# Output projections in the scores' single PSUM bank, maxima products and transposes in the triple, two products moved ahead of the scores

## The chip, the cores and the metric

The kernel runs on one core of one Trainium2 chip. A core has five engines that each work through a queue of their own in order: PE (TensorE, matrix products, with its weight loads shown as PEld), DVE (VectorE), ACT (ScalarE), POOL (GpSimd) and SP (SyncE), which here only issues the DMAs. PE writes its results to PSUM, eight banks of 512 float32 values on each of 128 partitions; DVE and ACT read them from there. The metric is the time of one execution in device microseconds. Before the change the median of three runs was 2083.55 us (2079.57 to 2088.34).

## The reference

Four layers in a row on one sequence of 2048 rows of 448 values: attention, feed-forward, attention, feed-forward, each behind a layer norm without weights and with a residual sum. The attention has 16 heads of 28 and one key and one value head for all; the feed-forward has 1792 hidden values. Both attentions share their weights, and so do both feed-forwards.

```
    def _A_ref(x, wq, wk, wv, wo):
        B, S, D = x.shape
        H = 16
        Dh = D // H
        q = (lambda x, *d: x.transpose(*d))((x @ wq).reshape(B, S, H, Dh), 0, 2, 1, 3)
        k = x @ wk
        v = x @ wv
        scores = jnp.einsum("bhqd,bkd->bhqk", q, k) * (Dh ** -0.5)
        p = _softmax(scores, axis=-1)
        o = jnp.einsum("bhqk,bkd->bhqd", p, v)
        return (lambda x, *d: x.transpose(*d))(o, 0, 2, 1, 3).reshape(B, S, H * Dh) @ wo
    def _B_ref(x, w_gate, w_up, w_down):
        g = _silu(x @ w_gate)
        u = x @ w_up
        return (g * u) @ w_down
    x = A_x
    x = x + _A_ref(_layernorm(x, axis=-1), A_wq, A_wk, A_wv, A_wo)
    x = x + _B_ref(_layernorm(x, axis=-1), B_w_gate, B_w_up, B_w_down)
    x = x + _A_ref(_layernorm(x, axis=-1), A_wq, A_wk, A_wv, A_wo)
    x = x + _B_ref(_layernorm(x, axis=-1), B_w_gate, B_w_up, B_w_down)
    return x
```

## The kernel before

The sequence is cut into four chunks of 512 rows (c = 0 to 3) and sixteen blocks of 128 keys (kt = 0 to 15). Products that must be precise are made of a high and a low part of each operand: three products of float32r values for one. All engines' orders are written out by hand: the order of the Python calls is the order of each engine's queue, and the framework adds the waits.

The function `forward` is called twice, with `full` false and, under a condition at the end that does not hold here, with `full` true. What follows is the first call.

**Projection stage (`project`, `q`, `finish`).** For each chunk four projections follow each other in the order `TURN`: first the one with the keys and values (m = 3), then the queries (m = 0, 1, 2), sixteen in all, counted by `seen`. Each is eleven matmuls in one of the banks 0 to 3. ACT copies the result, POOL (or, for m = 3, DVE at L453) takes the low half, and SP writes both halves to a DRAM tile `qd`; for m = 3 it also writes the keys (L131) and, from a DVE transpose into tile `sg` (L466), the values `vsb` (L468). The copies go through a ring of three buffers called `halves`. Ahead of each chunk's projections `turned` transposes the normalised rows `xn` of that chunk on PE (`flip`, L248); ACT and DVE take the transposes out of PSUM. For the last chunk the norm is applied (L230) behind projection 8 in layer 0, where `seen` is 8, and in layer 1 ahead of it; its transposes stand ahead of projection 11.

**Stacks.** A group i = (c, g) is one chunk of queries by four of the heads; there are sixteen in a layer. `stack(i)` reads the group's queries from `qd` into one of three tiles `qts` with four DMAs (L346). Stacks 0 and 1 are issued during the projections of chunk 0 and 1 (through the list `waiting`, one per projection), the others in the scores, at kt = 4 of two groups earlier.

**Maxima (`quick_steps`).** For each group a bound on the scores is taken: one product of the stacked queries with a few keys (`kdiag`, L362), a DVE transpose into `sg` (L364), a reduction (L366), a split in high and low (L368, L369), a transpose (L371), a cast into tile `down` (L373), and a DMA (L131) that writes the result into four rows of the group's `qts` tile. `down` and `sg` have one buffer each. The step of group 0 is run inside projection 7 by `tick`, which is called after every matmul of a projection and takes a step at every second call once `ready` allows it (`open`: when `seen` is over 6). The step of group i + 1 is run in group i.

**Scores (`scores`).** The eight banks are dealt anew: two triples (`threes`, three banks each, one tile each), bank 6 for the output of the attention, bank 7 as the single bank. One `step(n)` is one group by one block of keys: twelve score matmuls (L529), three banks of one triple and bank 7 for the fourth head, then two exps on ACT, first of bank 7 (`pt1`, L535), then of the triple (`pt`, L536). The triples take turns, bank 7 is used in every step. After each step comes `between_steps(n)`, then `pv(n - 2)`, the products of the exps with the values (L558). `between_steps` puts in what has to be done beside the scores, using the triple that the next step will write (`free`): at kt = 10 the maxima step of the next group in bank 0 of `free` and, where the list `todo` has some, an output projection (`outproj`: twelve matmuls at L515 and a DVE add into the residual at L519) in bank 1; from group 12 on a further output projection at kt = 13. In group 9, at kt = 4, 6, 8 and 10, it also puts in the transposes for the feed-forward's first chunk (`flip`, k = 0 to 3, in bank 2 of `free`), which DVE takes out in two passes (L251, L252; for k = 3 L255, L261).

`todo` gets the four projections of a chunk a few steps after the chunk's last group: of chunk 0 in group 4, of chunk 1 in group 8, of chunk 2 in group 12. So groups 4 to 11 have one at kt = 10, groups 12 and 13 have one at kt = 10 and one at kt = 13. Chunk 3's come after the scores.

**Feed-forward (`FeedForward`)** follows; in layer 0 it runs the first projections of the next attention between its last units.

## Time and profile before

| what | value |
|---|---|
| median of the runs | 2083.55 us |
| profiled execution, its own time | 2082.46 us |
| its span | 2080.7 us |
| PE busy | 2020.0 us |
| ACT busy | 1298.5 us |
| mean granted TensorE clock | 0.996 |
| maxima products in the scores | 30, in the projection stages 2 |
| output projections in the scores | 24 |
| scores, first step of layer 0 and of layer 1 on PE | 67.98 us and 1095.92 us |

The page gives busy times by engine, the chain that ended last, and groups of instructions by line, engine and tile. In a line of the timeline the first number is the start in us from the span's start, the second the duration in us, then engine, line, operation, tiles and shapes. A bracket at the end gives how long the engine sat idle before it and what ended that. In SP's lines the time is that of issuing, not of the transfer, and "x4" means four in a row. Ends of matmuls are modelled; starts are what the argument goes by.

### The profile page before, as it was taken

To read this page: it belongs to the slowest core of one execution; us is meant where nothing else is said; L and a number is where in the kernel's file an instruction comes from. 1 tells how busy PE (TensorE), PEld (TensorE's weight loads), DVE (VectorE), ACT (ScalarE), POOL (GpSimd) and SP (SyncE) were. 2 spreads that over 40 slices of the span, in tenths; PEclk is the share of its full clock that TensorE was granted. 3 is DMA by queue.
4 is the path that set the end of the run, shared out by engine and by line. 5 is a ranking of instruction groups with operands and counts; after the bars stand their busy time and mean duration, and the time that the engine had idled before them with its cause. 6 is when DMAs were issued, how large, how long until landed. Compare 5 with 4: busy or idle time off the path is not lost.

```text
span 2080.7 us, 43770 instructions
## 1 busy us (share of the span) xinstructions
PE 2020.0 (97%) x18577; PEld 1302.4 (63%) x18577; DVE 510.1 (25%) x1038; ACT 1298.5 (62%) x2126; POOL 493.3 (24%) x504
## 2 busy tenths in 40 slices
PE   7999999999999999999999999999999999999998
PEld 5433333333348999999883333333333589999997
DVE  6111112211114322223450110112121152223222
ACT  3799898788883333333338999897888643333332
POOL 5211101012202333332341110110222123333321
PEclk9999999999999999999999999999999999999999
DMA  6311010021100111100142110101121001111102
GB/s 197 104 36 36 20 27 20 16 45 31 36 7 23 30 30 30 30 16 26 36 130 64 30 38 16 30 16 30 31 42 24 12 18 31 30 30 30 30 2 74
DMA packets 86591, 78.24 MB, mean 38 GB/s; under 512 B 26736, under 2 KB 66032, under 8 KB 86384
## 3 DMA queue, kind: packets, MB, share of 16 engines
q1 hardware_dynamic: 86384, 75.33, 13.3%
q8 instruction: 148, 2.42, 0.5%
q14 instruction: 59, 0.48, 0.1%
HBM read 51.51 MB, written 18.61 MB: 34 GB/s over the span
## 4 chain that ended last, share of the span: by engine, by line
PE 51%; ACT 40%; DVE 3%; issue 2%; DMA 2%; SPq 1%; POOL 1%; ACTq 0%; DVEq 0%; POOLq 0%
PE bank L293 38%; ACT pt L536 27%; ACT pt L535 12%; PE three L515 3%; PE bank L271 3%; PE bank L558 2%; PE three L529 2%; PE bank L515 1%; PE three L362 1%; PE bank L248 1%; DVE sg L364 1%; DMA o<-rd 1%; DVE xl L252 1%; DVE stats L217 0%; SPq L131 0%
## 5 line engine op out<-in xcount | busy, mean ns | idle before, releaser
L536 ACT ACTIVATE pt<-three 128x1536 f32<-128x1536 f32 x512 | 741.6, 1448 | 0.0
L558 PE MATMUL bank<-pt,vsb 128*32 128x512 f32 x4096 | 545.9, 605 | 0.6 <-ACT pt L536 0.6
L529 PEld LDWEIGHTS three<-qstack,keys 32*128 32x128 f32 x4608 | 252.3, 183 | 454.7 <-ACT pt L535 388.2
L529 PE MATMUL three<-qstack,keys 32*128 32x512 f32 x4608 | 498.2, 425 | 7.5 <-DVE xl L252 3.5
L529 PE MATMUL bank<-qstack,keys 32*128 32x512 f32 x1536 | 492.0, 425 | 0.0
L293 PE MATMUL bank<-xh,wgh 64*128 64x512 f32 x1728 | 450.8, 390 | 0.5
L535 ACT ACTIVATE pt<-bank 128x512 f32<-128x512 f32 x512 | 306.1, 598 | 117.4 <-PE bank L529 115.9
L293 PE MATMUL bank<-xh,wgl 64*128 64x512 f32 x1404 | 369.7, 388 | 0.0
L293 PE MATMUL bank<-wdh,h 64*128 64x448 f32 x1792 | 335.2, 363 | 1.2 <-ACT h L767 0.9
L293 PE MATMUL bank<-xl,wgh 64*128 64x512 f32 x1296 | 335.0, 387 | 0.0
L293 PEld LDWEIGHTS bank<-xh,wgh 64*128 64x128 f32 x1728 | 267.7, 184 | 8.6 <-DVE xl L252 1.6
L592 POOL TENSOR_TENSOR o<-o 128x512 f32<-128x512 f32 x32 | 41.1, 1284 | 910.7 <-DMA o<-rd 649.7
L293 PEld LDWEIGHTS bank<-wdh,h 64*128 64x128 f32 x1792 | 249.0, 185 | 8.0 <-issue 2.5
L685 POOL TENSOR_TENSOR xres<-stage,xres 128x448 f32<-128x448 f32 x112 | 131.1, 1192 | 489.8 <-ACT stage L684 489.8
L529 PEld LDWEIGHTS bank<-qstack,keys 32*128 32x128 f32 x1536 | 243.6, 183 | 1.4 <-ACT pt L535 1.2
L300 ACT COPY seen<-bank 128x1 f32<-128x1 f32 x664 | 81.0, 164 | 239.7 <-PE bank L293 238.3
L293 PEld LDWEIGHTS bank<-xh,wgl 64*128 64x128 f32 x1404 | 220.8, 184 | 3.7
L293 PE MATMUL bank<-wdl,h 64*128 64x448 f32 x896 | 218.2, 365 | 0.0
L765 ACT ACTIVATE sg<-bank 128x512 f32<-128x512 f32 x112 | 67.1, 599 | 220.6 <-PE bank L293 211.1
L293 PEld LDWEIGHTS bank<-xl,wgh 64*128 64x128 f32 x1296 | 200.8, 185 | 2.7
L766 DVE TENSOR_TENSOR sg<-bank,sg 128x512 f32<-128x512 f32 x112 | 77.5, 692 | 495.1 <-ACT sg L765 486.1
L558 PEld LDWEIGHTS bank<-pt,vsb 128*32 128x32 f32 x4096 | 80.8, 108 | 186.3 <-issue 171.4
(115 smaller groups left out, 1723.0 us busy)
## 6 DMA issues: line engine op xcount, KB each, us to landing
qstack<-qd SPq DMA_DIRECT2D x128, 112.0 KB
qd<-q SPq DMA_DIRECT2D x24, 512.0 KB
o<-rd SPq DMA_DIRECT2D x32, 256.0 KB
wdr<-in_B_w_down_dram SPq DMA_DIRECT2D x28, 224.0 KB
wr<-in_B_w_gate_dram SPq DMA_DIRECT2D x28, 192.0 KB
wr<-in_B_w_up_dram SPq DMA_DIRECT2D x28, 192.0 KB
keys<-q SPq DMA_DIRECT2D x32, 112.0 KB
out_dram<-xres SPq DMA_DIRECT2D x16, 224.0 KB
```

What stands on the lines that cost most here:

```text
L271: nc.tensor.matmul(po, a, b, start=(i == 0), stop=(i == len(seq) - 1))
L293: nc.tensor.matmul(po, a, b, start=start, stop=stop, skip_group_check=True)
L300: nc.scalar.copy(seen[:, i : i + 1], po[:, 0:1])
L515: nc.tensor.matmul(po[:, 0:D], a[:, g, ts_], b[:, g, :], start=(g + z == 0), stop=(g == NG - 1 and z == 2))
L529: nc.tensor.matmul(three[:, j, :] if j < 3 else one, k[js, ks], q[js, part, :], start=(z == 0), stop=(z == 2), tile_position=(32 * j, 0),)
L535: nc.scalar.activation(pt1, one, AF.Exp, scale=SCALE)
L536: nc.scalar.activation(pt, three, AF.Exp, scale=SCALE)
L558: nc.tensor.matmul(accs[i][32 * j : 32 * j + 32, :], vsb[:, kt, :], pts[n][j], start=(kt == 0), stop=(kt == NT - 1), skip_group_check=True,)
L592: nc.gpsimd.tensor_tensor(rb, oraw, rb, ALU.mult)
L685: nc.gpsimd.tensor_tensor(r, s, r, ALU.add)
L765: nc.scalar.activation(sg, pg[0], AF.Silu)
L766: nc.vector.tensor_tensor(sg, pg[1], sg, ALU.mult)
```

## The change

There are five edits.

1. At kt = 10 the output projection goes to bank 7 (`one`) instead of bank 1 of the free triple; those at kt = 13 go to bank 0 of the triple.
2. The reading of the maxima product (now `rows`) and of the transposes (now `flipped`) is put on a list `behind` when in the scores. At kt = 10 PE's queue then has product, transposes, projection in this order, and DVE's has the maxima chain, the transposes' two passes, and the projection's add.
3. The transposes k = 0 to 3 move from kt = 4, 6, 8 and 10 of group 9 to kt = 10 of the groups 9, 10, 11 and 12.
4. The maxima steps of groups 0, 1 and 2 are all run in the projection stage, from projection 8 on (`seen` over 7) instead of that of group 0 in projection 7; in the scores the steps begin at group 2 (for group 3).
5. For that, stack 2 is issued in the projection stage too, behind the DMAs of projection 4, instead of at kt = 4 of group 0.

```
-    def flip(got, tiles, ks=range(4), place=None):
+    def flip(got, tiles, ks=range(4), place=None, behind=None):
...
+            if behind is None:
+                flipped(tiles, k, pt, nc.vector.tensor_copy if place is not None else nc.scalar.copy)
             else:
+                behind.append(lambda k=k, pt=pt: flipped(tiles, k, pt, nc.vector.tensor_copy))
+
+    def flipped(tiles, k, pt, copy):
+        xh, xl, xd = tiles
+        if k < 3:
+            copy(xh[:, k, :], pt)
+            nc.vector.tensor_tensor(xl[:, k, :], pt, xh[:, k, :], ALU.subtract)
+            return
+        if xd is None:
+            copy(xh[:, k, :], pt)
+            high = xh[64:128, k, :]
...
+        nc.vector.tensor_tensor(xh[64:128, k, :], pt[64:128, :], high, ALU.subtract)
...
             def one():
                 pm = self.mbank()[1]
                 nc.tensor.matmul(pm, kd.rearrange("p j k -> p (j k)"), q[:, 0, :], start=True, stop=True)
+                if self.lent is None:
+                    rows(pm)
+                else:
+                    self.behind.append(lambda: rows(pm))
+
+            def rows(pm):
                 side = pers.tile([P, 512], F32, name="sg")
                 nc.vector.transpose(side, pm)
...
-            if c == 0 and m < 2:
+            if c == 0 and m < 3:
                 self.waiting.append(lambda: self.stack(m))
...
-                self.ready = NM if self.seen > 6 else 0
+                self.ready = 3 * NM if self.seen > 7 else 0
...
-            self.advance(len(self.steps), NM + KC * LEAD if full else NM)
+            self.advance(len(self.steps), NM + KC * LEAD if full else 3 * NM)
...
                     free = threes[(n + 1) % 2]
+                    one = free[:, 1, :] if full else banks[7]
                     self.lent = free[:, 0, :]
-                    if full or kt == 10:
+                    if full or kt == 10 and i > 1:
                         self.advance(KC if full else 1)
...
-                    if todo and (kt == 10 or kt == 13 and i > 11):
-                        todo.pop(0)(free[:, 1, :])
-                    if i == 9 and kt in (4, 6, 8, 10):
-                        flip(got, X0, [kt // 2 - 2], free[:, 2, :])
+                    if kt == 10 and 8 < i < 13:
+                        flip(got, X0, [i - 9], free[:, 2, :], self.behind)
+                    while self.behind:
+                        self.behind.pop(0)()
+                    if todo and kt == 10:
+                        todo.pop(0)(one)
+                    elif todo and kt == 13 and i > 11:
+                        todo.pop(0)(free[:, 0, :])
...
-                    if kt == 4 and i + 2 < len(GR):
+                    if kt == 4 and 2 < i + 2 < len(GR):
                         self.stack(i + 2)
```

More of the change, by code (lines that the diff above doesn't have):

```diff
@@ L240, in norm @@
         return got
-    def flip(got, tiles, ks=range(4), place=None):
-        xh, xl, xd = tiles
+    def flip(got, tiles, ks=range(4), place=None, behind=None):
         for k in ks:
@@ L248, in flip @@
                 nc.tensor.transpose(pt[:, P * t : P * t + P], got["x"][:, t, P * k : P * k + P], ident)
-            copy = nc.vector.tensor_copy if place is not None else nc.scalar.copy
-            if k < 3:
-                copy(xh[:, k, :], pt)
-                nc.vector.tensor_tensor(xl[:, k, :], pt, xh[:, k, :], ALU.subtract)
-                continue
-            if xd is None:
-                copy(xh[:, k, :], pt)
-                high = xh[64:128, k, :]
-            else:
-                copy(xh[0:64, k, :], pt[0:64, :])
-                copy(xd[64:128, :], pt[64:128, :])
-                high = xd[64:128, :]
-            nc.vector.tensor_tensor(xh[64:128, k, :], pt[64:128, :], high, ALU.subtract)
+            if behind is None:
+                flipped(tiles, k, pt, nc.vector.tensor_copy if place is not None else nc.scalar.copy)
+            else:
+                behind.append(lambda k=k, pt=pt: flipped(tiles, k, pt, nc.vector.tensor_copy))
[9 more added lines that the diff above has]
+        else:
+            copy(xh[0:64, k, :], pt[0:64, :])
+            copy(xd[64:128, :], pt[64:128, :])
+            high = xd[64:128, :]
+        nc.vector.tensor_tensor(xh[64:128, k, :], pt[64:128, :], high, ALU.subtract)
     def product_T(po, a_h, a_l, tiles, tick=None):
@@ L313, in __init__ @@
             self.steps, self.places = [], []
-            self.lent, self.plan, self.waiting = None, {}, []
+            self.lent, self.plan, self.waiting, self.behind = None, {}, [], []
             for i in range(len(GR)):
@@ L362, in one @@
                 nc.tensor.matmul(pm, kd.rearrange("p j k -> p (j k)"), q[:, 0, :], start=True, stop=True)
+                if self.lent is None:
+                    rows(pm)
+                else:
+                    self.behind.append(lambda: rows(pm))
+            def rows(pm):
                 side = pers.tile([P, 512], F32, name="sg")
```

## The prediction

> **What bounds the kernel now.** I read the page first (busy times, then the chain that ended last), then the timeline of one outer stretch of the scores, then the DVE and SP timelines of the projection stage ahead of them. Of the page:

> ```profile
> PE 2020.0 (97%) x18577; PEld 1302.4 (63%) x18577; DVE 510.1 (25%) x1038; ACT 1298.5 (62%) x2126; POOL 493.3 (24%) x504
> PE 51%; ACT 40%; DVE 3%; issue 2%; DMA 2%; SPq 1%; POOL 1%; ACTq 0%; DVEq 0%; POOLq 0%
> ```

> PE is busy nearly throughout and ACT shares the chain with it only in the scores. The timeline of group 4, layer 0, shows two plain steps, and then what stands between steps 10 and 11, where maxima product and output projection are put:

> ```profile
> 207.85 0.50 PE L529 MATMUL three<-qstack,keys 32*128 32x512 f32 x3
> 209.75 0.51 PE L529 MATMUL three<-qstack,keys 32*128 32x512 f32 x3
> ...
> 212.72 0.60 ACT L535 ACTIVATE pt<-bank 128x512 f32<-128x512 f32 x1
> 212.82 0.50 PE L362 MATMUL three<-qstack,kdiag 128*128 128x512 f32 x1 [0.20 <-ACT pt L536]
> 213.36 0.72 DVE L364 STREAM_TRANSPOSE sg<-three 128x512 f32<-128x512 f32 x1 [11.38 <-PE three L362]
> 214.22 0.44 PE L515 MATMUL three<-woh,onh 128*128 128x448 f32 x1 [0.90 <-DVE sg L364]
> 215.50 0.18 DVE L373 CAST down<-flat 128x32 fp32r<-128x32 f32 x1
> 216.81 1.07 PE L558 MATMUL bank<-pt,vsb 128*32 128x512 f32 x8
> 216.92 0.62 DVE L519 TENSOR_TENSOR xres<-three,xres 128x448 f32<-128x448 f32 x1 [1.24 <-PE three L515]
> 217.81 0.51 PE L529 MATMUL three<-qstack,keys 32*128 32x512 f32 x3
> ```

> A plain step takes 1.90 us and PE is dense in it, so what is put between steps adds its PE time and its PE waits to the end. Here PE goes from the product (212.82) to step 11 (217.81) in 4.99 us. The avoidable part is ahead of 214.22: the projection writes the second bank of the triple, yet it waits until DVE has read the product out of the first (213.36+0.72). Reads and writes of one triple wait for each other whatever the bank.

> **The change, term by term.** *Output projection in bank 7.* It must wait for the exp that reads bank 7: 212.72+0.60=213.32, plus the few hundredths by which PE follows ACT, 213.38. That is 0.84 us ahead of 214.22. Nothing later takes it back: DVE ends the maxima chain at 215.68 (215.50+0.18), before the add is due (216.92-0.84=216.08); the add ends at 216.70, and step 11, which now waits for it through bank 7 only, is kept by pv until 216.97 anyway. This holds in groups 4 to 8 and 13: 6x0.84=5.0 us a layer. The projections at step 13 have no product ahead of them and only change bank of the triple: zero.

> *Two products leave groups 0 and 1.* Starts of the maxima's DVE transpose in layer 0, one per group:

> ```profile
> 151.10 0.72 DVE L364 STREAM_TRANSPOSE sg<-three 128x512 f32<-128x512 f32 x1 [11.29 <-PE three L362]
> 182.23 0.72 DVE L364 STREAM_TRANSPOSE sg<-three 128x512 f32<-128x512 f32 x1 [11.26 <-PE three L362]
> ...
> 317.35 0.72 DVE L364 STREAM_TRANSPOSE sg<-three 128x512 f32<-128x512 f32 x1 [11.24 <-PE three L362]
> 351.96 0.72 DVE L364 STREAM_TRANSPOSE sg<-three 128x512 f32<-128x512 f32 x1 [8.45 <-PE three L362]
> 391.13 0.72 DVE L364 STREAM_TRANSPOSE sg<-three 128x512 f32<-128x512 f32 x1 [3.66 <-PE three L362]
> 427.74 0.72 DVE L364 STREAM_TRANSPOSE sg<-three 128x512 f32<-128x512 f32 x1 [11.31 <-PE three L362]
> ```

> A group with a product takes 31.13 us against 16x1.90=30.4, so a product costs 0.75: 1.5 us a layer saved.

> *The transposes.* A group with product and projection takes 34.61 (317.35 to 351.96). The interval with the transposes of steps 4, 6 and 8 takes 39.17, 4.56 more; the one with those of step 10 takes 36.61, 2.00 more. Together 6.56 us a layer. One alone:

> ```profile
> 374.69 0.65 PE L248 MATMUL three<-ident,xn 128*128 128x128 f32 x4 [0.20 <-ACT pt L536]
> ...
> 376.17 0.69 DVE L252 TENSOR_TENSOR xl<-three,xh 128x512 fp32r<-128x512 f32 x1
> ...
> 376.92 0.50 PE L529 MATMUL three<-qstack,keys 32*128 32x512 f32 x3 [0.58 <-DVE xl L252]
> ```

> PE's part is about 0.5; the rest is the wait for two DVE passes of 0.69. After the change each of groups 9 to 12 has, between steps 10 and 11, product, transposes, projection. On the clock of group 4: transposes 213.2 to 213.8, projection from 213.7, pv ends at 217.3. DVE is now late: if its first read of the triple also waits for the transposes (as writes waited for reads above), the maxima chain of 2.32 us runs from 213.86 to 216.18, the two passes to 217.6, the add to 218.26, and step 11 starts at 218.32 against 217.81 before. So 4x0.51=2.0 us stay of 6.56: 4.5 saved a layer. If that read doesn't wait, step 11 starts at 217.84 and 6.4 are saved. I take the first, since the quoted wait shows the triple held as one.

> Scores: 5.0+1.5+4.5=11.0 a layer, 22.1 in both unrounded.

> *The projection stage pays.* Its cover is thin. Layer 0, DVE, then SP's queue, then PE and ACT:

> ```profile
> 46.92 0.72 DVE L364 STREAM_TRANSPOSE sg<-bank 128x512 f32<-128x512 f32 x1 [2.22 <-DMA vsb<-sg]
> 49.10 0.18 DVE L373 CAST down<-flat 128x32 fp32r<-128x32 f32 x1
> 49.20 0.68 DVE L453 TENSOR_TENSOR q<-bank,q 128x512 fp32r<-128x512 f32 x1
> 50.66 1.79 DVE L230 TENSOR_SCALAR xn<-xres,mv,rstd 128x448 f32<-128x448 f32 x4
> ```

> ```profile
> 35.94 2.15 SPq L346 DMA_DIRECT2D qstack<-qd  x4
> ...
> 42.45 2.60 SPq L468 DMA_DIRECT2D vsb<-sg  x4
> 45.15 1.05 SPq L458 DMA_DIRECT2D qd<-q  x2
> 49.35 0.62 SPq L131 DMA_DIRECT2D qstack<-down  x1
> ...
> 51.28 3.52 SPq L131 DMA_DIRECT2D keys<-q  x4
> ...
> 57.63 6.01 SPq L458 DMA_DIRECT2D qd<-q  x4
> ```

> ```profile
> 53.16 1.91 PE L248 MATMUL bank<-ident,xn 128*128 128x128 f32 x16
> ...
> 61.66 0.59 ACT L452 CAST q<-bank 128x512 fp32r<-128x512 f32 x1 [2.91 <-DMA qd<-q]
> ...
> 69.67 0.50 PE L529 MATMUL three<-qstack,keys 32*128 32x512 f32 x3 [0.72 <-ACT q L455]
> ```

> One maxima chain on DVE takes 2.36 us (46.92 to 49.28), and behind it in DVE's queue stand the low half of the keys' projection (49.20) and the norm of the last chunk (50.66), which PE transposes next (53.16). The changed kernel issues three chains back to back there, in projection 8. Tile `down` has one buffer, so each cast waits until the DMA before it has landed: SP 0.07+0.62, landing, cast 0.18. The landing isn't in the trace; the nearest row is the four small `vsb` DMAs, issued by 45.05 and landed by 46.92, 1.87 us. A link is then 2.74 us, and two links replace 49.28 by 54.76. The low half starts at 54.85 instead of 49.20 (+5.65), the norm ends at 58.1, PE's transposes start at 58.3 (+5.15). PE then idles over 4 us, and that costs clock as well, as in this stretch of layer 0's end (columns: PE, PEld, DVE, ACT, POOL busy, granted clock, DMA share, GB/s; the first row is the DMA load that counts below):

> ```profile
> 47.00:48.00 1.00, 1.00 (x6) 0.81 (x5) 0.97 (x2) 0.00 (x0) 0.92 (x2) 1.00 0.98 383
> 1034.00:1035.00 1.00, 0.00 (x0) 0.00 (x0) 0.80 (x2) 0.29 (x3) 0.00 (x0) 1.00 0.00 0
> 1037.00:1038.00 1.00, 1.00 (x7) 0.67 (x5) 0.23 (x1) 0.58 (x1) 0.00 (x0) 0.50 0.00 0
> ```

> After that idle time the clock was 0.50 for some 3.3 us: 1.65 lost. PE had 0.72 to spare before step 1 (69.67), so layer 0 loses 5.15+1.65-0.72=6.1. SP's queue comes close: it is 5.0 late from the keys (51.28) on, and the stage already ends through it (61.66 waits for the DMA issued at 57.63). The third stack's four issues (2.15 in the row at 35.94) move ahead of the two at 45.15 and fall into SP's idle time up to 49.35: no cost of their own beyond the DMA load. The stack's landing, about 49.1 (45.1+2.15+1.87), holds the third product back some 2 us, which lies under the 4 us that PE waits later.

> Layer 1:

> ```profile
> 1071.91 0.70 DVE L261 TENSOR_TENSOR xh<-bank,xh 64x512 fp32r<-64x512 f32 x1
> ...
> 1078.21 0.68 DVE L453 TENSOR_TENSOR q<-bank,q 128x512 fp32r<-128x512 f32 x1
> ```

> Here the norm stands ahead of the chains, so PE loses less: from 1072.61, norm 1.79, chain 2.36, half a microsecond for one more `qd` issue on SP, two links 5.5, so the low half starts near 1082.8 (+4.6), and the stage ends through SP's queue that much later. The stages lose 6.1+4.6=10.7.

> **Sum.** The profiled execution took 2082.46 us (span 2080.7); 2082.46-22.1+10.7=2071.1. It lies 1.09 below the median of 2083.55 of the runs shown; I keep its scale. A measurement of this kernel tells about 0.5%, 10.4 us, from no change.

> **Bounds.** Stages: if the landing hides under the next chain, the links shrink to 2.36, and without the clock loss the stages lose 7.5. With the better reading of the transposes the scores save 26: 2082.46-26+7.5=2064.

> **Rivals.** *Cheap stages and free transposes*: 2064. For it: nothing shows the landing of `down`. Against: the triple is held as one in every quoted wait. Chance 0.15.

> *`down` lands behind the big writes.* After the change the two `qd` writes of 45.15 are issued from 47.3 and a third from 48.4, and they load the DMA engines fully (0.98 in the row above, 512 KB each, 1.4 us each at 383 GB/s). If their bytes start 1 us after the issue, as I estimate, they run until about 52.6; the first `down` is issued at 49.35. If it lands after them, with 1.2 for the landing at 53.8, the first link grows by 2 us: layer 0 loses 8, layer 1 5.4, and the time is 2073.8. Chance 0.22. [...]

> *The wait is only exchanged.* The projection still starts at 214.22, because bank 7 or its operands are held by something that the sg row covers. The 10.1 us of that term are lost: 2081.2. Against it: the exp ends at 213.32. Chance 0.08.

> *Slower: the links decide.* The longest landing that the chain of waits shows is

> ```profile
> 342.13 5.81 DMA o<-rd
> ```

> If each `down` took 5.81 from its issue, a link would be 6.06, four of them 13.3 more than taken: 2084.4, above before. It decides from a link of 5.6 us on (10.7+4x(5.6-2.74)=22.1); with the clock loss in layer 1 too it passes 2086. Chance 0.10.

> **How the numbers follow.** The forecast has 0.45. Of it about two thirds lie below 2073.1 (0.5% under the median), of the ring-order case a quarter, of the cheap case all: 0.30+0.05+0.15, with its spread 0.53 faster. The slower side beyond 0.5% is a part of the last rival and what I haven't seen: 0.09. The rest, 0.38, is within 0.5%. Range 2062 to 2082, from the cheap case to the exchanged wait; the likeliest case's own is 2068 to 2074.

> **What would show it.** The first L515 row of groups 4 to 8 about 0.55 us behind its product, held by ACT's pt L535; group intervals of 33.8; 30.4 for groups 0 and 1; one transposes' row in each of groups 9 to 12 with step 11 held by DVE's add or xl. [...] Wrong would be: a projection that still waits for sg, a read of the triple that doesn't wait for the transposes, or casts 6 us apart.

## The result, and the profile after

The changed kernel took 2075.78 us in the median (2073.92 to 2077.32, five runs), beside 2083.55 (2079.57 to 2088.34, five runs too) before: a ratio of 0.9963 with the 95% interval 0.9946 to 0.9981. That is a gain of 7.8 us where 11.4 was forecast (2082.46 to 2071.1), inside the 10.4 us (0.5%) that were set as the bound of "no change": the prediction gave this outcome 0.38, and 0.53 to a larger gain. The interval lies below 1, so the gain is clear of the noise. The profiled execution took 2076.66 (span 2074.9), 5.8 less than that of before.

The profile page after, the lines of busy times and of the chain that ended last by engine:

```profile
PE 2024.9 (98%) x18577; PEld 1303.5 (63%) x18577; DVE 507.9 (24%) x1038; ACT 1301.0 (63%) x2126; POOL 492.2 (24%) x504
PE 48%; ACT 44%; DVE 3%; issue 2%; SPq 2%; DMA 1%; POOL 0%; ACTq 0%; DVEq 0%
```

The work is the same. The chain has moved from PE (51% before) to ACT (40% before), and it did so in the scores; SP's queue has gone from 1% to 2%, and the rise is in the projection stages.

To see where the 5.8 us come from, both executions are cut at the same places: the first transposes on PE, the first exp of a layer, the DVE transposes of the maxima in groups 4 and 13, the table load behind the last exp, and, as the start of layer 1, the load of the exp table.

| stretch | before, us | after, us | difference | forecast |
|---|---|---|---|---|
| layer 0, start to first transposes | 9.46 | 10.30 | +0.84 | 0 |
| layer 0, projection stage, to the first exp | 60.05 | 67.67 | +7.62 | +6.1 |
| layer 0, first exp to group 4 | 143.85 | 144.99 | +1.14 | -1.5 |
| layer 0, group 4 to group 13 | 321.15 | 312.38 | -8.77 | -8.7 |
| layer 0, group 13 to the end of the scores | 79.40 | 78.88 | -0.52 | -0.84 |
| layer 0, feed-forward | 447.77 | 446.53 | -1.24 | 0 |
| layer 1, projection stage, to the first exp | 36.51 | 41.70 | +5.19 | +4.6 |
| layer 1, first exp to group 4 | 145.63 | 144.95 | -0.68 | -1.5 |
| layer 1, group 4 to group 13 | 321.16 | 312.43 | -8.73 | -8.7 |
| layer 1, group 13 to the end of the scores | 79.42 | 78.77 | -0.65 | -0.84 |
| layer 1, feed-forward to the end | 436.30 | 436.30 | 0 | 0 |

The forecast for groups 4 to 13 is five projections of 0.84 (the sixth lies behind group 13) and the 4.5 of the transposes. The middle of the scores did what was said; the beginning of the scores and the projection stages did not. The timeline of group 4, layer 0:

```profile
222.42 0.50 PE L368 MATMUL three<-qstack,kdiag 128*128 128x512 f32 x1 [0.21 <-ACT pt L548]
222.96 0.72 DVE L376 STREAM_TRANSPOSE sg<-three 128x512 f32<-128x512 f32 x1 [11.38 <-PE three L368]
223.06 0.44 PE L527 MATMUL bank<-woh,onh 128*128 128x448 f32 x1
...
225.65 1.06 PE L575 MATMUL bank<-pt,vsb 128*32 128x512 f32 x8
225.83 0.62 DVE L531 TENSOR_TENSOR xres<-bank,xres 128x448 f32<-128x448 f32 x1 [0.56 <-PE bank L527]
...
226.65 0.51 PE L541 MATMUL three<-qstack,keys 32*128 32x512 f32 x3
```

The projection (223.06) no longer waits for the DVE transpose of the product and starts 0.64 us behind the product (1.40 before). Step 11 follows the product by 4.23 us instead of 4.99: 0.76 saved, 0.84 forecast. Group 9, where the transposes have come in, holds all three things:

```profile
392.06 0.51 PE L368 MATMUL three<-qstack,kdiag 128*128 128x512 f32 x1 [0.20 <-ACT pt L548]
392.41 0.60 PE L248 MATMUL three<-ident,xn 128*128 128x128 f32 x4
...
392.76 0.45 PE L527 MATMUL bank<-woh,onh 128*128 128x448 f32 x1
...
393.12 0.72 DVE L376 STREAM_TRANSPOSE sg<-three 128x512 f32<-128x512 f32 x1 [12.00 <-PE three L248]
...
396.06 0.69 DVE L258 TENSOR_TENSOR xl<-three,xh 128x512 fp32r<-128x512 f32 x1
...
396.81 0.50 PE L541 MATMUL three<-qstack,keys 32*128 32x512 f32 x3 [0.38 <-DVE xl L258]
```

DVE's first read of the triple did wait for the transposes (393.12 is released by L248, not by the product), as taken, and step 11 follows the product by 4.75 where 5.50 was worked out. Of the 3.63 us from DVE's first read (393.12) to its last (396.06+0.69) 2.25 lie beside the projection's twelve matmuls, which end where pv starts, at 395.37.

The projection stage of layer 0, DVE first, then SP's queue:

```profile
49.04 0.72 DVE L376 STREAM_TRANSPOSE sg<-bank 128x512 f32<-128x512 f32 x1 [2.03 <-DMA vsb<-sg]
...
51.22 0.18 DVE L385 CAST down<-flat 128x32 fp32r<-128x32 f32 x1
...
55.63 0.18 DVE L385 CAST down<-flat 128x32 fp32r<-128x32 f32 x1 [2.22 <-DMA qstack<-down]
...
57.96 0.18 DVE L385 CAST down<-flat 128x32 fp32r<-128x32 f32 x1
58.06 0.69 DVE L465 TENSOR_TENSOR q<-bank,q 128x512 fp32r<-128x512 f32 x1
...
59.53 1.78 DVE L230 TENSOR_SCALAR xn<-xres,mv,rstd 128x448 f32<-128x448 f32 x4
```

```profile
49.20 1.96 SPq L470 DMA_DIRECT2D qd<-q  x3
51.47 7.27 SPq L131 DMA_DIRECT2D qstack<-down  x3
58.84 0.65 SPq L470 DMA_DIRECT2D qd<-q  x1
59.55 3.46 SPq L131 DMA_DIRECT2D keys<-q  x4
```

Three chains stand back to back, and the low half of the keys' projection starts at 58.06 instead of 49.20. Of these 8.86 us two links make 6.74, the later start of the program 0.84, and 1.28 arose ahead of the first chain. The first link, from one cast to the next, is 4.41 us (51.22 to 55.63), the second 2.33. The first is near what the rival with `down` behind the big writes gave (4.74), the second is nearly the chain itself: DVE waits 0.14 us for the DMA there. In layer 1 the casts stand at 1075.84, 1080.13 and 1083.02.

The casts aren't the only thing that holds this stage. The chain that ended last passes here by another way in layer 0, through the third stack and PE:

```profile
48.72 2.81 DMA qstack<-qd
...
51.66 0.47 PE bank L368
52.14 5.26 PE bank L277 x16
...
57.47 0.60 ACT q L467
58.07 0.69 DVE q L465
```

The third product waits 1.84 us for the third stack (landed at 51.5, where the prediction had 49.1), PE's clock is then 0.50 from 52.1 to 55.5, and ACT's copy of the keys' projection ends at 58.07, as late as DVE's three chains. The prediction had put the stack at no cost, under 4 us of PE waiting ahead of its last transposes; PE waited 0.31 us there. In the repetition e0 it waited 2.04, and the chain that ended last passes both the stack's landing and the two landings of `down`; in layer 1 of both profiles it passes a landing of `down`. So two paths stand close to each other in layer 0, and the links are the longer one only in some executions.

What the sum did not have stands at the start of the scores. The windows of 1 us there (PE, PEld, DVE, ACT and POOL busy, granted clock, DMA share, GB/s), and the two waits of PE ahead of them:

```profile
79.00:80.00 1.00, 0.69 (x12) 0.18 (x4) 0.00 (x0) 1.00 (x2) 1.00 (x1) 0.69 0.62 216
80.00:81.00 1.00, 1.00 (x7) 0.76 (x11) 0.00 (x0) 1.00 (x2) 0.13 (x1) 0.50 1.02 373
85.00:86.00 1.00, 1.00 (x12) 0.20 (x8) 0.00 (x0) 0.34 (x1) 0.00 (x0) 0.50 0.00 0
...
1105.00:1106.00 1.00, 1.00 (x11) 0.67 (x9) 0.00 (x0) 1.00 (x2) 0.00 (x0) 0.50 1.00 391
```

```profile
78.12 0.50 PE L541 MATMUL three<-qstack,keys 32*128 32x512 f32 x3 [1.36 <-ACT q L467]
```

```profile
1102.61 0.51 PE L541 MATMUL three<-qstack,keys 32*128 32x512 f32 x3 [3.06 <-ACT q L467]
```

Step 1 of the scores waits until ACT has copied the last projection out of its bank, 1.36 us in layer 0 and 3.06 in layer 1, and behind that the granted clock is 0.50 for about 7 us in each layer. That copy itself waited 3.45 and 4.00 us for the keys' DMAs, late in SP's queue; by the code it needs one of the three buffers of `halves` back. Before, layer 0's wait was 0.72 with no drop, and layer 1's was 1.45 with one of 3 us.

### The profile page after: what moved, and what is told of

Same layout as the page of the kernel before. It is cut to its first block, busy times and chain, and to the rows that moved or that the text cites. A ratio compares the mean times of both kernels' runs of the same rounds, so it can differ in the third digit from the quotient of the medians.

```text
span 2074.9 us, 43753 instructions
## 1 busy us (share of the span) xinstructions
PE 2024.9 (98%) x18577; PEld 1303.5 (63%) x18577; DVE 507.9 (24%) x1038; ACT 1301.0 (63%) x2126; POOL 492.2 (24%) x504
## 4 chain that ended last, share of the span: by engine, by line
PE 48%; ACT 44%; DVE 3%; issue 2%; SPq 2%; DMA 1%; POOL 0%; ACTq 0%; DVEq 0%
PE bank L299 38%; ACT pt L548 29%; ACT pt L547 14%; PE bank L527 3%; PE bank L277 3%; PE three L541 1%; PE bank L575 1%; PE bank L248 1%; PE bank L541 1%; SPq L131 1%; PE three L527 1%; DVE xl L258 0%; DVE xn L230 0%; DVE stats L217 0%; PE three L368 0%
## 5 line engine op out<-in xcount | busy, mean ns | idle before, releaser
L299 PE MATMUL bank<-xh,wgh 64*128 64x512 f32 x1728 | 470.9, 390 | 0.5
L299 PE MATMUL bank<-xh,wgl 64*128 64x512 f32 x1404 | 382.3, 388 | 0.0
L299 PE MATMUL bank<-xl,wgh 64*128 64x512 f32 x1296 | 350.1, 387 | 0.0
L299 PE MATMUL bank<-wdh,h 64*128 64x448 f32 x1792 | 339.5, 362 | 1.3 <-ACT h L784 0.9
L299 PEld LDWEIGHTS bank<-xh,wgh 64*128 64x128 f32 x1728 | 287.2, 184 | 8.9 <-DVE xl L258 1.6
L299 PEld LDWEIGHTS bank<-wdh,h 64*128 64x128 f32 x1792 | 263.0, 184 | 7.7 <-issue 2.7
L299 PEld LDWEIGHTS bank<-xh,wgl 64*128 64x128 f32 x1404 | 235.3, 184 | 4.1
L299 PE MATMUL bank<-wdl,h 64*128 64x448 f32 x896 | 228.0, 364 | 0.0
L299 PEld LDWEIGHTS bank<-xl,wgh 64*128 64x128 f32 x1296 | 215.4, 185 | 2.8
```

What stands on the lines that cost most here:

```text
L299: nc.tensor.matmul(po, a, b, start=start, stop=stop, skip_group_check=True)
```

## The experiments

The runs stand beside runs of the kernel before on the same chip (medians 2084.5 to 2084.8). Stages are of each one's profiled execution.

| kernel | median us | ratio, 95% interval | stage 0 | scores 0 | feed-forward 0 | stage 1 | scores 1 |
|---|---|---|---|---|---|---|---|
| before | 2083.55 | 1 | 60.05 | 544.40 | 447.77 | 36.51 | 546.21 |
| changed | 2075.78 | 0.9963 (0.9946 to 0.9981) | 67.67 | 536.25 | 446.53 | 41.70 | 536.15 |
| e0 changed, again | 2077.9 | 0.9967 (0.9955 to 0.9979) | 65.71 | 533.73 | 447.91 | 41.65 | 536.23 |
| e1 bank 7 alone | 2068.53 | 0.9927 (0.9914 to 0.994) | 60.40 | 537.39 | 449.12 | 36.01 | 536.40 |
| e2 products unmoved | 2067.80 | 0.992 (0.9906 to 0.9934) | 60.23 | 535.92 | 447.98 | 36.07 | 535.24 |
| e3 three buffers for `down` | 2071.25 | 0.9938 (0.9925 to 0.9952) | 62.63 | 535.26 | 448.10 | 39.80 | 535.92 |
| e4 transposes spread alone | 2114.85 | 1.0149 (1.0133 to 1.0166) | 59.90 | 562.70 | 447.88 | 36.21 | 560.78 |
| e5 write ahead of `down` | 2078.78, one run | | 66.61 | 535.36 | 447.92 | 43.73 | 537.26 |
| e6 products one each | 2075.97 | 0.9959 (0.9946 to 0.9973) | 61.26 | 538.18 | 448.02 | 42.99 | 536.26 |
| e7 e6 with three buffers | 2074.72 | 0.9952 (0.9938 to 0.9966) | 61.94 | 537.96 | 448.03 | 42.63 | 536.23 |
| e8 e7, own value tile | 2060.61 | 0.9888 (0.9872 to 0.9904) | 62.31 | 533.83 | 445.41 | 40.50 | 534.30 |
| e9 e2, own value tile | 2061.78 | 0.989 (0.9874 to 0.9906) | 60.73 | 535.25 | 444.63 | 36.55 | 538.19 |
| e10 PE kept busy | 2074.35 | 0.995 (0.9936 to 0.9964) | 67.98 | 534.01 | 449.20 | 41.69 | 533.66 |
| e11 changed, own value tile | 2072.24 | 0.9943 (0.9927 to 0.996) | 67.84 | 533.76 | 445.66 | 41.53 | 535.70 |

The theory at the start: the scores gain, mostly through bank 7, and the chains in the projection stages take part of it back. The first rival: the transposes are a gain of their own, and the moved products are cheap.

**e0, the changed kernel again.**

> The changed kernel once more, beside the others on the same chip: 2074 to 2078 us by its five runs. If the clock is 0.5 again for several us behind step 1 of the scores in both layers, the slow clock belongs to the kernel; if it is gone or elsewhere, it is variation.

It came out as before, 0.9967. Layer 0's stage was 2 us shorter than in the first profile and layer 1's the same; so layer 0's loss is 5.7 to 7.6 us and layer 1's 5.2. The 2 us lie ahead of the chains: the first cast stands 38.72 us behind the first transposes, 40.92 in the first profile and 39.64 before. The clock is 0.50 again in layer 1 (1100 to 1107), but not at the start of layer 0's scores; there it stands at 59 to 63 instead, on the last transposes of the stage.

**e1, bank 7 alone.** The kernel before, with one edit:

```
-                        todo.pop(0)(free[:, 1, :])
+                        todo.pop(0)(free[:, 1, :] if full or kt == 13 else banks[7])
```

> The kernel before with one edit: the projections at step 10 go to bank 7. Theory (the wait for DVE's reading of the product is gone, nothing else changes): groups with product and projection shrink from 34.6 to 33.9 us, ten groups a layer, 20 x 0.73 = 14.6 us less, near 2069 us on the scale of 2083.55. Rival (the wait is only exchanged for the exp or the add): under 4 us less. The projection stages should be as before (first exp of layer 0 within 2 us of 69.5).

Measured 2068.53, as expected, and 8 to 9 us under the changed kernel on the same chip (e0; 8.3 by the ratios, 9.4 by the medians). One line gives more than the five edits together. Its groups 4 to 13 take 314.71 and 313.84 us, so that 6.4 and 7.3 of the 8.7 us saved there come from the bank.

**e2, the products unmoved.** The changed kernel with the second and third product back in groups 0 and 1, and stack 2 back at kt = 4 of group 0:

```
-            if c == 0 and m < 3:
+            if c == 0 and m < 2:
...
-                self.ready = 3 * NM if self.seen > 7 else 0
+                self.ready = NM if self.seen > 6 else 0
...
-            self.advance(len(self.steps), NM + KC * LEAD if full else 3 * NM)
+            self.advance(len(self.steps), NM + KC * LEAD if full else NM)
...
-                    if full or kt == 10 and i > 1:
+                    if full or kt == 10:
...
-                    if kt == 4 and 2 < i + 2 < len(GR):
+                    if kt == 4 and i + 2 < len(GR):
```

> The changed kernel with the products of groups 1 and 2 back in the scores, the product of group 0 back in projection 7 and stack 2 back in group 0. Theory (the moved products cost some 11 us in the two stages and a slow clock at the scores' start of some 5 us, and save 3 us): some 12 us under the changed kernel, near 2063 us. Rival (the stages' loss in the profile is variation of the start, and the moved products save what they take out of the scores): 3 us over the changed kernel, near 2079 us.

Measured 2067.80, 10 us under the changed kernel on the same chip (e0), where 12 were expected: moving the products loses 10 us net. Both stages are those of the kernel before (60.23 and 36.07). Beside e1 the spread transposes add 1.5 us in layer 0's scores and 1.2 in layer 1's, not 4.5. (These two figures come from one profile of each kernel; the medians, 0.7 us apart, don't tell the two kernels apart.)

**e3, three buffers for `down`.** The changed kernel with one edit:

```
-                down = pers.tile([P, 32], F32R, name="down")
+                down = pers.tile([P, 32], F32R, name="down", bufs=3)
```

> The changed kernel with three buffers for the tile of the maxima's DMA, so that no cast waits for a DMA. Theory (the first link waits 2.2 us for a DMA that lands behind the big writes): the three casts 2.2 us apart, the last one 2.2 us earlier than in the changed kernel in each layer, 4 us or a little more less in all, near 2071 us; the DVE chains stay, so it does not come near the kernel with the products unmoved. Rival (SP's queue or the third stack's DMA sets the end, not the casts): as the changed kernel.

Measured 2071.25, as expected, and 6 to 7 us under e0. No cast waits for a landing any more:

```profile
48.35 0.18 DVE L385 CAST down<-flat 128x32 fp32r<-128x32 f32 x1
...
50.58 0.18 DVE L385 CAST down<-flat 128x32 fp32r<-128x32 f32 x1
...
52.80 0.18 DVE L385 CAST down<-flat 128x32 fp32r<-128x32 f32 x1
52.90 0.68 DVE L465 TENSOR_TENSOR q<-bank,q 128x512 fp32r<-128x512 f32 x1
```

The links are the bare chain, 2.23 and 2.22 us. So the landing was 2.2 us of the first link and nearly nothing of the second, and 2.6 us of the loss stay in layer 0's stage without it (62.63 against 60.05).

**e4, the transposes spread alone.** The changed kernel with e2's edits, and with the projections back in the second bank of the triple:

```
-                    one = free[:, 1, :] if full else banks[7]
+                    one = free[:, 1, :]
```

> The changed kernel without its first two parts: the output projections stay in the second bank of the triple, behind the evacuation of the maxima product, and the second and third products stay in groups 0 and 1; only the transposes are spread over groups 9 to 12, at step 10. Theory (the gain of the scores belongs to bank 7, and the spreading is worth little or nothing by itself): in the kernel before, one set of transposes between steps 10 and 11 cost 2.00 us, and the other three 4.56 together; four at that place cost 8.0 against 6.56, a loss of 1.4 us a layer, 2.9 us in both: ratio about 1.001, 2087 against a before of 2084. Rival 1 (the prediction's term: the spreading saves 4.5 us a layer whatever the projection's bank): ratio 0.9957, 2075. Rival 2 (what it added to bank 7 alone, 1.2 to 1.5 us a layer, is its own): ratio 0.9987, 2081.

All three expectations missed: 30 us slower than before. Group 10, layer 0, in the timeline, and windows of it (columns as above):

```profile
427.34 0.51 PE L368 MATMUL three<-qstack,kdiag 128*128 128x512 f32 x1 [0.20 <-ACT pt L548]
427.68 0.60 PE L248 MATMUL three<-ident,xn 128*128 128x128 f32 x4
...
431.34 0.69 DVE L258 TENSOR_TENSOR xl<-three,xh 128x512 fp32r<-128x512 f32 x1
432.08 0.74 PE L527 MATMUL three<-woh,onh 128*128 128x448 f32 x1 [3.80 <-DVE xl L258]
...
438.10 0.50 PE L541 MATMUL three<-qstack,keys 32*128 32x512 f32 x3
```

```profile
431.00:432.00 1.00, 0.00 (x0) 0.00 (x0) 0.96 (x2) 0.00 (x0) 0.00 (x0) 0.50 0.00 0
436.00:437.00 1.00, 1.00 (x7) 0.46 (x9) 0.03 (x1) 0.00 (x0) 0.00 (x0) 0.50 0.00 0
438.00:439.00 1.00, 1.00 (x16) 0.50 (x12) 0.00 (x0) 0.00 (x0) 0.00 (x0) 1.00 0.00 0
```

The projection, now a writer of the triple, stands behind every reader of it: the maxima chain's first pass and both passes of the transposes. PE is idle for 3.80 us, the clock falls to 0.50, and the projection runs at that clock. Step 11 comes 10.76 us behind the product. Group 10 takes 40.41 us, where the changed kernel takes 34.91. So the spreading, with the projection behind the transposes as edit 2 puts it, has no gain of its own: in that order it needs bank 7 first. The spreading with the projection ahead of the transposes was not run. The expectation of 2087 took "the first row of transposes at this place" as the price of four, but in that row of before the projection was ahead of the transposes in PE's queue, and here it is behind them.

**e5, a write ahead of the first `down`.** The changed kernel with 448 KB more on SP's queue:

```
+                if i == 0:
+                    spare = dram.tile([P, 2 * D], F32, name=f"spare{self.layer}")
+                    nc.sync.dma_start(spare, xres[:, 0:2, :].rearrange("p t d -> p (t d)"))
                 dma(q[28:125:32, :, :].rearrange("j z (b w) -> j (z b) w", w=32), down)
```

> The changed kernel with one more write of 448 KB from SBUF to HBM on SP's queue, just ahead of the first small down DMA of each layer's projection stage; it computes the same, and the bytes written are read by nobody. Theory (the small DMA lands behind the bytes that were issued ahead of it on the same queue): the first link, from the first to the second down cast, grows from 4.41 us in layer 0 and 4.29 us in layer 1 by 1.2 us for the bytes at 383 GB/s and up to 0.4 us for the later issue, to 5.6 to 6.0 us and 5.5 to 5.9; the second link stays at 2.3 and 2.9. Rival (the small DMA has a landing time of its own and the first link was long for another reason, for instance the late third stack): only the later issue shows, 4.4 to 4.8 us in both layers.

Layer 0, DVE:

```profile
48.19 0.18 DVE L385 CAST down<-flat 128x32 fp32r<-128x32 f32 x1
...
53.70 0.18 DVE L385 CAST down<-flat 128x32 fp32r<-128x32 f32 x1 [3.32 <-DMA qstack<-down]
...
56.09 0.18 DVE L385 CAST down<-flat 128x32 fp32r<-128x32 f32 x1 [0.21 <-DMA qstack<-down]
```

The first link is 5.51 us (4.41 without the write), in layer 1 6.02 (4.29), and the second links are 2.39 and 2.43. Both first links lie just outside the ranges expected (5.6 to 6.0 and 5.5 to 5.9), but far above the rival's 4.4 to 4.8. Without the write, the other executions of this stage have 4.53 and 4.57 in layer 0, 4.02 and 4.24 in layer 1 (e0, e10). So the first landing moves with the bytes ahead of it, by about 1 us in layer 0 and 1.7 to 2 in layer 1, and the second hardly moves (2.33 to 2.39) or gets shorter (2.89 to 2.43). Here, then, the small DMA lands behind the big writes that were issued before it. The changed kernel shows the same without the extra write: its DMA engines were full (busy share 1.04 in the mean) from 50.75 to 54.5 in layer 0 and from 1074.25 to 1078.25 in layer 1, and the casts that wait for the first `down`, issued from 51.47 and 1076.12 on, came at 55.63 and 1080.13. The time of this single run is not compared.

**e6, one product each in projections 12 to 14.** The changed kernel with one edit:

```
-                self.ready = 3 * NM if self.seen > 7 else 0
+                self.ready = NM * max(0, min(3, self.seen - 11))
```

> The changed kernel with its three maxima products ahead of the scores spread out: one each in projections 12, 13 and 14 instead of all three in projection 8; groups 0 and 1 stay without one. Theory (the stages lose because three chains stand back to back in DVE's queue ahead of the low half and the norm, and because the start of the scores finds a PE that has idled): both projection stages come back to within 1 us of the kernel before, 60 to 61 and 36 to 37 us from the first transposes to the first exp, no slow clock stands at the start of the scores, and the time is 2 to 4 us under that of the kernel with the products unmoved, which was 2067.8: about 2065, ratio 0.9905. Rival 1 (a product and its chain cost as much in the stage as in the scores, wherever they are put): 2068, ratio 0.992. Rival 2 (the third stack's early issue and the queue of SP hold the stage, not the chains): the stages stay 3 us or more longer than before, 2073 or more, ratio 0.994 or more.

Measured 2075.97: no gain over the changed kernel, the time of rival 2, with layer 0's stage only 1.2 us longer than before and layer 1's 6.5. No PE or DVE row of these stages waits for the third stack. Two rows of layer 0:

```profile
72.97 0.72 DVE L376 STREAM_TRANSPOSE sg<-bank 128x512 f32<-128x512 f32 x1 [7.76 <-DMA vsb<-sg]
```

```profile
73.83 0.80 PE L541 MATMUL three<-qstack,keys 32*128 32x512 f32 x3 [3.71 <-DVE sg L376]
```

What decides is a wait that stood in no expectation. The second chain waits 7.76 us for the DMAs that carry the transposed values out of tile `sg`, since chain and values share that tile, and those DMAs stand late in SP's queue (68.94 to 71.56). Step 1 of the scores waits for the chain, and the clock falls again (0.50 from 74 to 80). In layer 1 the stage is 42.99.

**e7, e6 with three buffers for `down`.**

> The kernel with one product each in projections 12, 13 and 14, and with three buffers instead of one for the tile down. Theory (with a projection's time between the chains the small DMA has landed before the next cast, so that its buffer is no limit): the same time as with one buffer, within 1 us. Rival (each landing still holds DVE for some of the time, as the 1.9 us a landing did when the chains stood back to back): 1 to 3 us faster.

2074.72 beside 2075.97: 1.25 us, just inside the rival's range, with intervals that overlap. The profile of e6 decides: none of its `down` casts waits more than 0.23 us for a landing, so `down` is no limit there.

**e8, e7 with the values in a tile of their own.** One line, a tile that is idle at that time:

```
-            vt = pers.tile([P, 512], F32, name="sg")[64:96, :]
+            vt = wpool.tile([P, 4, 2, P], F32, name="wr").rearrange("p k b n -> p (k b n)")[64:96, 0:512]
```

> The kernel with one product each in projections 12, 13 and 14 and three buffers for down, with one more edit: the transposed values, which the maxima chains shared the tile sg with, get another tile (that of the raw weights, idle at that time), so that a chain no longer waits until the vsb DMAs have read the values out of sg. Theory (that wait is what cost the products their gain there: DVE idle for 7.75 us in layer 0, step 1 of the scores held 3.71 us by the sg row, and then the clock at 0.50): the second chain starts some 7 us earlier, step 1 no longer waits for DVE, about 6 us come back in layer 0 and 4 to 6 in layer 1, 2063 to 2066, ratio about 0.990. Rival (the chains then stand behind something else, as the landing of down behind the big writes on SP, or DVE's low half): 2070 or more, ratio 0.993 or more.

2060.61, 13 to 14 us under e7 and below the 2063 to 2066 expected: 0.9888 (0.9872 to 0.9904). With e9 it is the fastest; the two can't be told apart. The two profiled executions are 10.0 us apart: 4.1 in layer 0's scores, 2.6 in its feed-forward, 2.1 in layer 1's stage and 1.9 in its scores, and nothing in layer 0's stage, where the expectation had much of it. The second chain starts at 66.92 instead of 73.85 (e7), step 1 waits 0.34 for ACT and no longer for DVE, and there is no drop of the clock at the start of the scores in either layer. From the first exp to group 4 it takes 142.46 and 142.44 us; e2, with the two products inside, 143.91 and 143.88. That is the saving of the moved products as forecast: 1.45 of 1.5.

**e9, e2 with the values in a tile of their own** (the same line).

> The kernel with the products unmoved (two of them in groups 0 and 1, one ahead of the scores), with the transposed values in a tile of their own. Theory (the shared tile costs the stage also where only one product stands in it: its chain waits 1.99 us for the vsb DMAs in layer 0): the low half and the norm behind the chain come 2 us earlier, the stage ends through SP's queue 1 to 2 us earlier in each layer, 2064 to 2066, ratio about 0.9905. Rival (something else sets the stage's end, such as the big qd writes on SP): no difference, 2067.8, ratio 0.992.

The time is a little below the expectation, 2061.78, but not for the reason given: the stages are not shorter (60.73 and 36.55), the feed-forward of layer 0 is, by 3.35 us. The tile `sg` is also the one that the feed-forward's silu is written into, and the first projections of the next layer run between its last units. ACT, in e2 and then in e9:

```profile
1024.24 0.60 ACT L782 ACTIVATE sg<-bank 128x512 f32<-128x512 f32 x1 [4.29 <-DMA vsb<-sg]
```

```profile
1022.36 0.60 ACT L782 ACTIVATE sg<-bank 128x512 f32<-128x512 f32 x1 [1.96 <-PE bank L299]
```

In e2 the silu waits for the values' DMAs, and the clock falls to 0.50 from 1029 to 1032 behind it; in e9 it waits for its own product, and that drop is gone. In the three kernels with an own tile that stage takes 444.6 to 445.7 us, in all others 446.5 to 449.2. The two medians are 6.0 us apart; the profiled executions show 3.35 of it, and e9's gives 2.95 back in layer 1's scores, where the clock fell behind a wait of 1.49 us, so that the two spans are equal. What the medians show beyond that is not accounted for.

**e10, PE kept busy.** The changed kernel, with products between step 0 and step 1 that nobody reads; it computes more than is needed and the same result:

```
                     step(n)
+                    if n == 0 and not full:
+                        for _ in range(13 if self.layer else 5):
+                            nc.tensor.matmul(
+                                banks[6], qts[0][:, 0, 0:128], qts[0][:, 0, :], start=True, stop=True
+                            )
                     between_steps(n)
```

> The changed kernel with products that nobody reads, put on PE between step 0 and step 1 of the scores, five in layer 0 (1.1 us) and thirteen in layer 1 (3.0 us), into the accumulators' bank, which the first pv overwrites; they fill the 1.36 and 3.06 us in which PE waits there for ACT. Theory (those waits are what drops the granted clock to 0.50 in the first steps of the scores, for about 7 us in each layer): the windows behind the first exp show 1.00, the scores of each layer lose some 3 us, 2069 to 2071, ratio 0.993 to 0.994. Rival (the clock drops for what lies further back, the idle time inside the projection stage): the windows stay at 0.50 and the time stays within 1.5 us of the changed kernel's, ratio 0.996 to 0.997.

The windows behind the first exp are at full clock in both layers:

```profile
80.00:81.00 1.00, 0.85 (x11) 0.49 (x12) 0.00 (x0) 1.00 (x2) 0.13 (x1) 1.00 1.02 375
...
1105.00:1106.00 1.00, 1.00 (x12) 0.52 (x12) 0.00 (x0) 1.00 (x2) 0.03 (x1) 1.00 1.00 373
```

From the first exp to group 4 it now takes 142.59 and 142.46 us, 2.4 and 2.5 less than in the changed kernel. The mechanism is as the theory had it in layer 1, where every other run with three products in projection 8 has a drop at that place (between 1095 and 1113). In layer 0 it is not settled by this run: e0 and e11 have no drop there either, and theirs, like this one's, lies in the projection stage at 59 to 64. The time, 2074.35, lies between the two expectations: by the ratios it is 2.7 us under the changed kernel and 3.5 under its repetition e0, where the scores' share would be 4.9. The intervals overlap, so the windows and the stretches show the effect, and the time alone does not.

**e11, the changed kernel with an own value tile.**

> The changed kernel, its three products still in projection 8, with the transposed values in a tile of their own. Theory (the three chains back to back, and the first down behind the big qd writes, are what its stages lose, and the shared tile only adds what it adds everywhere): the gain is that of the kernel with the products unmoved, which went from a ratio of 0.992 to 0.989 by the same edit; here from 0.9965 to 0.9935, 2071; in layer 0 the first chain starts some 2 us earlier and the second down cast comes no earlier, since it waits for the same writes. Rival (the shared tile was also what the changed kernel's stages lost): ratio 0.990 or less, 2064 or less.

2072.24, as the theory had it. In layer 0 the first chain no longer waits for the values, but 1.66 us for its own product, so that its cast comes 0.8 us earlier (50.45) and not 2; the second cast comes at 54.91, and the link of 4.46 is as long as with the shared tile; stage 0 stays at 67.84. So the shared tile is a cost beside the chains, not theirs, as long as the chains stand in projection 8.

## Why the prediction was right or wrong

*The size.* 2071.1 was forecast against the profiled execution of before, 2076.66 was measured in the profiled execution after: 5.6 us less gain. Of that 2.1 lie in the stages (12.8 lost, 10.7 forecast) and 3.9 in the scores (18.2 saved, 22.1 forecast); the start of the program (+0.84) and the feed-forward (-1.24) give 0.4 back. The rival with `down` behind the big writes, 2073.8, was nearer than the forecast; its losses of 8 and 5.4 us in the stages were nearly those measured (7.62 and 5.19).

*Output projection in bank 7.* Right, a little too large: 0.76 in group 4 instead of 0.84. The rival by which the wait is only exchanged is out: the projection's row names no wait at all.

*The transposes.* Right as a sum with the former, wrong as a term of its own; that the whole of groups 4 to 13 came out says nothing for this term. Groups 4 to 13 were forecast 8.7 us shorter and are 8.77 and 8.73 shorter. But in groups 9 to 12 the projection too had moved to bank 7, and the forecast put what that saves into the transposes' term. e1 shows the bank alone at 6.4 to 7.3 of the 8.7, e1 and e2 together show the spreading at 1.2 to 1.5 a layer, and e4 shows it at 18.3 and 14.6 us the other way without the bank. In the row of group 9 its mechanism is as forecast: DVE's first read waits for the transposes, and step 11 waits 0.38 us for their second pass.

*Two products leave groups 0 and 1.* The mechanism is right: 1.45 a layer in e8 against e2, of 1.5. In the changed kernel itself it does not show, since the start of the scores runs at half the clock: +1.14 and -0.68 in place of -1.5 each.

*The clock.* This is the step that failed by most. The forecast had one loss of 1.65 us, for PE's transposes in layer 0 behind 4 us of idle time. In the changed kernel's first profile the clock is 1.00 there (58 to 64); it is 0.50 there in e0, e5, e10 and e11, so this term is borne out in four of the five profiles with three chains in projection 8 and one buffer. What the forecast lacked stands elsewhere: one stretch of 3.4 us at 0.50 behind the wait for the third stack (52.1 to 55.5), and two stretches of about 7 us at 0.50 at the start of the scores, some 2.5 us each by e10; before, one of 3 us stood there. The latter are the 3.5 us between the forecast for the two stretches up to group 4 (-3.0) and what was measured (+0.46), nearly all that the scores fell short by. The prediction asked of each stage how late its end comes; it did not ask how long PE waits between step 0, for which everything is there, and step 1, which is held by ACT's late copy.

*The projection stage pays: the link.* The mechanism is right in layer 1 and in e0, and the term was mis-sized. "A link is then 2.74 us" was worked out from a landing of 1.87. The first link is 4.41 and 4.29 us, the second 2.33 and 2.89, in sum 6.74 and 7.18 instead of 5.5. The rival with `down` behind the big writes, the ring-order case of the chances, had the first link nearly right (4.74). It took 1 us from the issue to the first bytes, which agrees with the trace of before: two `qd` writes issued from 45.15 on, and the DMA engines full from 46.25. The 1.2 us that it took for the landing was the author's estimate; after, the cast came 1.1 and 1.9 us behind the end of the full load. The ring order of that name is shown by no run; what the runs show is that the first landing came later with more bytes ahead of it on SP's queue, with links of 4.41 and 4.29 us in the changed kernel and 5.51 and 6.02 in e5. This rival had a chance of 0.22, though the three writes of 512 KB ahead of the small DMA stood in the prediction already. With three buffers (e3) layer 0's stage is 3.1 us shorter than in e0, whose first cast stands nearly as early (38.72 us behind the first transposes, 38.27 in e3), and layer 1's is 1.9 shorter: the landing is about half of layer 0's loss and a third of layer 1's. The rest was not taken apart; the chains themselves and what stands behind them on DVE and SP are in it.

*The third stack: no cost.* Wrong in layer 0. It landed at 51.5 instead of 49.1, and the PE time that was to hide this, 4 us of waiting ahead of the last transposes, was 0.31 us in the first profile and 2.04 in e0. The chain that ended last passes this landing in both. No run has the three products in projection 8 with an earlier stack, so its price by itself stays open.

*The slower rival, links of 6.06.* Out: no link of the changed kernel passes 4.57.

*The wait of the first chain* for `vsb<-sg`, 2.22 us in the row of before that the prediction quotes and 2.03 after, was taken as given. Another tile for the values was worth 6 us beside e2 (e9), 5 to 6 beside e0 (e11) and 13 to 14 beside e7 (e8), though in e9 not by this wait, since its stages got no shorter.

## What to carry to other kernels

Split the price of an edit by the resource that it frees, and ask of each part whether it is worth anything without the other: bank 7 alone was worth more than all five edits, and the transposes' new place and order, without it, cost 30 us. Work put ahead of a loop, into time that looks idle, costs by its queues (7.62 and 5.19 us of the stages here): look at what the small DMA stands behind, and which tile with one buffer is shared with a transfer. Where a row says `<-DMA` ahead of a write into a tile and that DMA reads the tile, as `vsb<-sg` does (2.03 us in the changed kernel, 7.76 in e6), the write waits for a transfer out of it, and another tile for one of its two users may be all that is wanted.

## What the runs showed of the hardware

```profile
75.96:79.37 3.41, 2.05 (x24) 0.99 (x24) 0.00 (x0) 1.89 (x3) 1.55 (x3) 1.00 0.29 52
79.37:82.79 3.42, 3.11 (x17) 1.32 (x20) 0.00 (x0) 3.03 (x5) 0.76 (x1) 0.50 0.99 369
```

- A window did not have to be idle to be followed by a drop here: some in which PE was busy for up to 69% were. What tells those between 49 and 69% apart stays open.
- A small DMA (16 KB) from SBUF to SBUF took 4.0 to 4.6 us from cast to cast behind three writes of 512 KB on the same queue (after, e0, e10), 5.5 and 6.0 with 448 KB more ahead of it (e5), and 2.3 to 2.4 in layer 0 with no further write ahead (second link), where the chain without a wait takes 2.2 (e3).
- Where a drop of the clock falls varies between executions of the same kernel: from 45 us on, layer 0 of the changed kernel had it at 52 to 55 and 79 to 86 in one profile and at 59 to 63 in the other.
